# A gated mix of linear attention and a SwiGLU block: the first half of a weight load changes its DMA queue, and one dummy product is dropped

## The chip, the core and the metric

The kernel runs on one core of a Trainium2 chip. The metric is the device time of one execution in microseconds (us). A profile is one further execution of the same program, with a record for each instruction and each DMA.

## The reference

Two branches read the same x and are mixed by a gate for each token. Cut to what matters (S = 2048 tokens, D = 512, F = 1376, 32 heads of 16; all inputs bf16):

```python
g = sigmoid((x * gate_w).sum(-1, keepdims=True))
# A: linear attention, phi(t) = where(t > 0, t + 1, exp(t)) + 1e-6
q, k, v = split(x @ wqkv)                     # each S x 512
kv  = einsum("bhsd,bhse->bhde", phi(k), v);  z = phi(k).sum(over tokens)
a   = (phi(q) @ kv / (phi(q) . z + 1e-6)) @ wo
# B: SwiGLU
b   = (silu(x @ w1) * (x @ w3)) @ w2
out = g * a + (1 - g) * b
```

## The kernel before, in words

The tokens are cut into 16 tiles of 128 (`t`), four tiles to a block of 512 (`tb`). A product on TensorE needs x transposed, with the feature on the partition; this copy is `xT`. Almost all of `xT` is made by transposing DMAs straight from HBM (lines 89 and 93). Only the first two tiles, the "x pair", come in plainly (line 84, 256 KB into `x_sb`) and are turned on TensorE by `emit_xT` (line 176): eight transposes into PSUM, which VectorE (line 181) and ScalarE (line 183) copy into `xT`.

The start of the kernel goes in this order:

- Dummy products (`emit_warm`, line 163) on constants keep TensorE busy while the first loads travel: six of 512 columns and three of 128.
- The eight transposes of the x pair, line 176.
- The k products of tiles 0 to 3 (`emit_k_mm`, line 186): four for each tile, one for each 128-row chunk `kc` of the weight `wk_sb`. The order of the first eight is written out by hand: chunks 0 and 1 of tile 0, chunks 0 and 1 of tile 1, then chunks 2 and 3 of tile 0 and of tile 1. So the first four need only the first half of `wk_sb` (line 85), the next four the second half (line 86). Tiles 2 and 3 read the `xT` that the transposing DMA of line 89 brings.
- From tile 4 on, TensorE alternates between `emit_xp` of tile u (line 206, which reads `x_sb` of tile u) and the k products of tile t. Tiles 2 to 7 of `x_sb` come in one DMA of 768 KB (line 98), and the first of them is wanted by the third `emit_xp`.

After that come the q products, the gate and remainder columns (line 243), the SwiGLU products (lines 312 and 320) and the output products (lines 348 to 357), block by block.

TensorE's order is the order of the program, since the kernel asks for a manual schedule of that engine. Each DMA is issued by an engine's instruction queue, in the order of that queue. All loads but one are issued from SyncE (SP), the exception being line 85, which ScalarE issues:

```python
dq = nc.sync
dq.dma_start(out=x_sb[:, 0:TF, :], in_=x_first)
nc.scalar.dma_start(out=wk_sb[:, 0:2, :], in_=wqkv_r[:, 0:2, D : 2 * D])
dq.dma_start(out=wk_sb[:, 2:4, :], in_=wqkv_r[:, 2:4, D : 2 * D])
```

The whole function:

Of the kernel before, what the change touches and what calls it, by code (L numbers as in the profile page):

```python
# [17 lines left out]
def kernel(  # L18
# [12 lines left out]
    nc = tc.nc  # L31
    P = nc.NUM_PARTITIONS

    Bb, S, D = A_x.shape
# [5 lines left out]
    TB = 512  # L40
# [25 lines left out]
    wk_sb = consts.tile([P, KC, D], BF16, name="wk_sb")  # L66
# [9 lines left out]
    wqkv_r = A_wqkv.rearrange("(kc d) n -> d kc n", d=P)  # L76
# [3 lines left out]
    dq = nc.sync  # L80
# [1 line left out]
    x_first = x2d[0 : TF * P, :].rearrange("(p j) d -> p j d", j=TF)  # L82
    out_first = out2d[0 : TF * P, :].rearrange("(p j) d -> j p d", j=TF)
    dq.dma_start(out=x_sb[:, 0:TF, :], in_=x_first)
    nc.scalar.dma_start(out=wk_sb[:, 0:2, :], in_=wqkv_r[:, 0:2, D : 2 * D])
    dq.dma_start(out=wk_sb[:, 2:4, :], in_=wqkv_r[:, 2:4, D : 2 * D])
    pre = consts.tile([1, 1], FP32, name="pre")
    nc.scalar.activation(out=pre[:], in_=nc.const_aps.tensor(0.0, [1, 1], FP32), func=ACT.Exp)
# [1 line left out]
        out=xT[:, :, TF * P : TB], in_=x2d[TF * P : TB, :], transpose=True  # L90
    )
    for tb in range(1, NTB):
        dq.dma_start(
            out=xT[:, :, tb * TB : (tb + 1) * TB], in_=x2d[tb * TB : (tb + 1) * TB, :],
# [7 lines left out]
    with nc.allow_non_contiguous_dma(reason="one gate weight per partition and chunk"):  # L102
        dq.dma_start(
            out=wr_sb[:, :, 2 * FR : NR], in_=gate_w.rearrange("(kc d o) -> d kc o", d=P, o=1)
# [7 lines left out]
    for fcs in (slice(0, FC // 2), slice(FC // 2, FC)):  # L112
# [9 lines left out]
        out=bm, in_=bm, pattern=[[-Dh, HPC], [0, Dh]], compare_op=ALU.is_ge, fill=0.0,  # L122
# [3 lines left out]
        out=bm, in_=bm, pattern=[[Dh, HPC], [0, Dh]], compare_op=ALU.is_ge, fill=0.0,  # L126
# [33 lines left out]
    def emit_warm(*widths):  # L160
        warm = psX.tile([P, TB], FP32, tag="XP3", name="warm")
        for n in widths:
            nc.tensor.matmul(  # L163
                warm[:, 0:n], lhsT=warm_l, rhs=warm_r[:, 0:n], start=True, stop=True
            )

    emit_warm(TB, TB, TB, TB, TB, TB, P, P, P)

    st = {}

# [244 lines left out]
    for c in range(KC):  # L415
# [7 lines left out]
        out=kvT_sb[:], in0=kvT_ps[:],  # L423
# [65 lines left out]
```

## Time and profile before

| what | value |
|---|---|
| median of 4 runs | 179.68 us (178.89 to 180.21) |
| the profiled execution's own time | 179.26 us |
| its span, from the first to the last instruction | 177.5 us |
| time of that execution outside the span | 1.76 us |
| TensorE busy | 173.0 us, 97% of the span |
| VectorE, ScalarE, GpSimd busy | 66%, 37%, 36% |
| moved by DMA | 15.14 MB, mean 85 GB/s over the span |
| of it from ScalarE's DMA queue (q10) | 0.26 MB |

The span is counted from zero at the first instruction. PE stands for TensorE's products, PEld for its weight loads, which run beside the products; a weight load that waits is named with what it waited for. SPq and ACTq are the DMA-issuing instructions of SyncE and ScalarE; their duration is the time that the issuing engine spends on the instruction, and the time to landing runs from the start of the issue to the last byte's report.

### The profile page before, as it was taken

How to read it: one execution, taken by the hardware profiler on the slowest of the kernel's cores; microseconds unless marked ns; L12 is line 12 of the kernel's file. 1: busy time of each engine (PE TensorE's matmuls, PEld its weight loads, DVE VectorE, ACT ScalarE, POOL GpSimd, SP SyncE). 2: the span in 40 equal slices, each digit the busy share in tenths (PEclk: the TensorE clock that was granted, in tenths of full speed). 3: DMA queues.
4: the chain of work that ended last, by engine and by line, in shares of the span. 5: the costliest groups of instructions: out<-in, count | busy, mean ns of one | idle time of the engine just before them, and what ended most of it. 6: DMA issues, size and time to landing. Idle time of an engine off the chain costs nothing.

```text
span 177.5 us, 2453 instructions
## 1 busy us (share of the span) xinstructions
PE 173.0 (97%) x868; PEld 83.8 (47%) x884; DVE 117.8 (66%) x203; ACT 65.9 (37%) x124; POOL 63.3 (36%) x71
## 2 busy tenths in 40 slices
PE   8999999999999999999999999999999999999993
PEld 4444444474445454444454544444545444444463
DVE  0596858898998637597776466878754668776000
ACT  3624224466433333333244333243434323341222
POOL 5197655958262323262003232710032328000000
PEclk9999999999999999999999999999999999999999
DMA  5999999921014011124000111230002022200011
GB/s 170 230 305 246 234 344 361 350 77 28 9 30 91 7 41 37 37 59 89 0 4 7 40 33 37 71 78 6 0 7 67 7 70 59 59 0 0 30 36 56
DMA packets 30252, 15.14 MB, mean 85 GB/s; under 512 B 20672, under 2 KB 30112, under 8 KB 30240
## 3 DMA queue, kind: packets, MB, share of 16 engines
q1 hardware_dynamic: 29968, 14.72, 30.5%
q10 hardware_dynamic: 272, 0.26, 0.4%
q8 instruction: 7, 0.11, 0.3%
q14 instruction: 5, 0.04, 0.1%
HBM read 8.42 MB, written 2.10 MB: 59 GB/s over the span
## 4 chain that ended last, share of the span: by engine, by line
PE 97%; issue 1%; DVE 0%; DVEq 0%
PE o_ps L357 19%; PE up_ps L320 19%; PE gate_ps L312 19%; PE o_ps L348 8%; PE XP L206 8%; PE q_ps L219 8%; PE k_ps L186 6%; PE r_ps L243 3%; PE k L186 2%; PE o_ps L352 2%; PE warm L163 2%; PE kvT_ps L418 1%; PE W_ps L440 0%; PE xTp L176 0%; PE z_ps L431 0%
## 5 line engine op out<-in xcount | busy, mean ns | idle before, releaser
L312 PE MATMUL gate_ps<-xT,w_sb 128*128 128x512 bf16 x157 | 40.7, 379 | 0.1
L320 PE MATMUL up_ps<-xT,w_sb 128*128 128x512 bf16 x157 | 40.6, 379 | 0.2
L227 POOL TENSOR_TENSOR qz<-pq,z_sb 128x512 f32<-128x512 bf16 x16 | 18.5, 1164 | 59.6 <-DVE pq L147 58.4
L325 ACT ACTIVATE th<-gate_ps 128x512 bf16<-128x512 f32 x40 | 23.9, 597 | 37.9 <-PE gate_ps L312 36.4
L357 PE MATMUL o_ps<-w_sb,hT 128*128 128x512 bf16 (+3 forms) x177 | 37.3, 355 | 0.2
L327 DVE SCALAR_TENSOR_TENSOR gs<-th,gate_ps 128x512 bf16<-128x512 bf16 x40 | 27.3, 683 | 5.6 <-ACT th L325 5.3
L330 DVE TENSOR_TENSOR hT<-up_ps,gs 128x512 bf16<-128x512 f32 x40 | 27.6, 691 | 3.7
L144 DVE TENSOR_SCALAR phi_m<-phi_e 128x512 bf16<-128x512 bf16 x32 | 14.1, 441 | 21.4 <-ACT phi_e L142 21.3
L357 PEld LDWEIGHTS <-hT 128*128 128x128 bf16 x180 | 16.8, 98 | 17.9
L320 PEld LDWEIGHTS <-w_sb 128*128 128x128 bf16 x160 | 15.7, 98 | 18.9
L312 PEld LDWEIGHTS <-w_sb 128*128 128x128 bf16 x160 | 15.6, 98 | 18.6
L362 ACT ACTIVATE o_out<-o_ps,omg 128x512 bf16<-128x512 f32 (+2 forms) x17 | 11.2, 659 | 30.8 <-PE o_ps L357 30.8
L292 POOL TENSOR_TENSOR pqn<-pq,rden 128x512 bf16<-128x512 bf16 x16 | 16.6, 1057 | 14.0 <-DVE rden L285 11.7
L196 POOL TENSOR_TENSOR pks<-pks,pk_sb 128x512 f32<-128x512 f32 x15 | 17.5, 1165 | 7.3 <-DVE pk_sb L147 6.7
L348 PE MATMUL o_ps<-W_sb,pqT 128*128 128x512 bf16 (+3 forms) x70 | 16.7, 354 | 0.1
L230 DVE TENSOR_REDUCE den<-qz 128x32 f32<-128x512 f32 x16 | 11.0, 685 | 8.6 <-POOL qz L227 8.5
L206 PE MATMUL XP<-pk_sb,x_sb 128*128 128x512 bf16 x62 | 16.2, 379 | 0.1
L219 PE MATMUL q_ps<-wq_sb,xT 128*128 128x512 bf16 x61 | 16.1, 379 | 0.1
L142 ACT ACTIVATE phi_e<-k_ps 128x512 bf16<-128x512 f32 x12 | 7.2, 597 | 14.4 <-PE k_ps L186 14.4
L142 ACT ACTIVATE phi_e<-q_ps 128x512 bf16<-128x512 f32 x16 | 9.6, 597 | 7.8 <-PE q_ps L219 6.7
L186 PE MATMUL k_ps<-wk_sb,xT 128*128 128x512 bf16 x48 | 12.3, 379 | 0.0
L147 DVE SCALAR_TENSOR_TENSOR pq<-q_ps,phi_m 128x512 bf16<-128x512 f32 x16 | 11.1, 691 | 0.5
(59 smaller groups left out, 117.1 us busy)
## 6 DMA issues: line engine op xcount, KB each, us to landing
w_sb<-in_B_w_dram SPq DMA_DIRECT2D x6, 640.0 KB, 8.5
out_dram<-o_out SPq DMA_DIRECT2D x15, 128.0 KB, 1.9
x_sb<-in_A_x_dram SPq DMA_DIRECT2D x2, 512.0 KB, 4.2
x_sb<-in_A_x_dram SPq DMA_DIRECT2D x1, 768.0 KB, 5.0
wq_sb<-in_A_wqkv_dram SPq DMA_DIRECT2D x1, 512.0 KB, 6.1
wv_sb<-in_A_wqkv_dram SPq DMA_DIRECT2D x1, 512.0 KB, 6.7
wo_sb<-in_A_wo_dram SPq DMA_DIRECT2D x1, 512.0 KB, 10.1
wk_sb<-in_A_wqkv_dram ACTq DMA_DIRECT2D x1, 256.0 KB, 3.5
```

The costliest lines, as they stand in the source:

```text
L186: nc.tensor.matmul(k_ps[:], lhsT=xT[:, kc, t * P : (t + 1) * P], rhs=wk_sb[:, kc, :], start=(kc == 0), stop=(kc == KC - 1),)
L196: nc.gpsimd.tensor_add(pks[:], pks[:], pk_sb[:, t, :])
L206: nc.tensor.matmul(XP_ps[dc][:], lhsT=x_sb[:, t, dc * P : (dc + 1) * P], rhs=pk_sb[:, t, :], start=(t == 0), stop=(t == NT - 1),)
L219: nc.tensor.matmul(q_ps[:], lhsT=xT[:, kc, ts_tok], rhs=wq_sb[:, kc, :], start=(kc == 0), stop=(kc == KC - 1),)
L227: nc.gpsimd.tensor_tensor(out=qz[:], in0=st[tb, "pq"][:, tt, :], in1=z_sb[:], op=ALU.mult)
L312: nc.tensor.matmul(gate_ps[:], lhsT=w1_sb[:, kc, fsl], rhs=xT[:, kc, tok_sl], start=(kc == 0), stop=(kc == KC - 1),)
L320: nc.tensor.matmul(up_ps[:], lhsT=w3_sb[:, kc, fsl], rhs=xT[:, kc, tok_sl], start=(kc == 0), stop=(kc == KC - 1),)
L325: nc.scalar.activation(out=th[:], in_=gate_ps[:], func=ACT.Tanh, scale=0.5)
L327: nc.vector.scalar_tensor_tensor(out=gs[:], in0=th[:], scalar=1.0, in1=gate_ps[:], op0=ALU.add, op1=ALU.mult)
L330: nc.vector.tensor_tensor(out=st[tb, "hT"][:, fc, :], in0=up_ps[:], in1=gs[:], op=ALU.mult)
L348: nc.tensor.matmul(o_ps[:], lhsT=st[tb, "pqT"][:, c, tsl], rhs=W_sb[:, c, a:b], start=(c == 0), stop=False,)
L357: nc.tensor.matmul(o_ps[:], lhsT=st[tb, "hT"][:, fc, tsl], rhs=w2_sb[:, fc, a:b], start=False, stop=(fc == FC - 1),)
```

## The change

The DMA that loads the first half of `wk_sb` is issued by SyncE instead of ScalarE. In SyncE's queue it stands second, behind the x pair and ahead of the second half of `wk_sb`; whatever SyncE issues after it comes one instruction later than before. The list of dummy products loses one of its three 128-column members.

```diff
     dq.dma_start(out=x_sb[:, 0:TF, :], in_=x_first)
-    nc.scalar.dma_start(out=wk_sb[:, 0:2, :], in_=wqkv_r[:, 0:2, D : 2 * D])
+    dq.dma_start(out=wk_sb[:, 0:2, :], in_=wqkv_r[:, 0:2, D : 2 * D])
     dq.dma_start(out=wk_sb[:, 2:4, :], in_=wqkv_r[:, 2:4, D : 2 * D])
...
-    emit_warm(TB, TB, TB, TB, TB, TB, P, P, P)
+    emit_warm(TB, TB, TB, TB, TB, TB, P, P)
```

## The prediction

> **What bounds the kernel now.** I read the page's chain first, then the start of the span weight load by weight load, then SyncE's DMA issues, then the landings. All of the change lies in the first microseconds; the chain says whether they count.
>
> ```profile
> PEclk9999999999999999999999999999999999999999
> ...
> PE 97%; issue 1%; DVE 0%; DVEq 0%
> ```
>
> The chain that ended last is TensorE's work, almost without a break. So a microsecond that TensorE loses at the start reaches the end in full, and one that it gains does too, if no later load makes it wait. The clock row is for the section on rules below.
>
> The timeline of the weight loads shows what TensorE waits for at the start (start us, length us, line, count, idle before it and its releaser):
>
> ```profile
> 2.93 0.15 PEld L163 LDWEIGHTS <-const-bfloat16-1.0 128*128 128x128 bf16 x1 [0.28 <-issue]
> 3.36 0.25 PEld L163 LDWEIGHTS <-const-bfloat16-1.0 128*128 128x128 bf16 x2 [0.28 <-issue]
> 3.77 0.65 PEld L176 LDWEIGHTS <-x_sb 128*128 128x128 bf16 x8 [0.15 <-DMA x_sb<-in_A_x_dram]
> 4.55 0.11 PEld L186 LDWEIGHTS <-xT 128*128 128x128 bf16 x2
> 4.86 1.10 PEld L186 LDWEIGHTS <-xT 128*128 128x128 bf16 x6 [0.20 <-DVE xT L181]
> 6.32 1.41 PEld L186 LDWEIGHTS <-xT 128*128 128x128 bf16 x8 [0.36 <-DMA xT<-in_A_x_dram]
> ```
>
> Two loads end waits of TensorE: the x pair at 3.77 and the first transposing DMA at 6.32. The second is the one to keep in mind. Between them lie the eight k products of tiles 0 and 1, from 4.55 on, at 0.216 each (the chain has four products of line 206 at 0.86): 4.55 + 8 x 0.216 = 6.28. TensorE and that DMA arrive together, within 0.04; the 0.36 is the idle time of the weight loader, not of the array.
>
> SyncE's DMA issues, in order of time:
>
> ```profile
> 0.81 0.40 SPq L84 DMA_DIRECT2D x_sb<-in_A_x_dram  x1
> 1.27 0.41 SPq L86 DMA_DIRECT2D wk_sb<-in_A_wqkv_dram  x1
> 1.73 1.32 SPq L89 DMA_TRANSPOSE xT<-in_A_x_dram  x1
> 3.10 2.89 SPq L93 DMA_TRANSPOSE xT<-in_A_x_dram  x1
> 6.03 0.58 SPq L98 DMA_DIRECT2D x_sb<-in_A_x_dram  x1
> 6.66 4.17 SPq L93 DMA_TRANSPOSE xT<-in_A_x_dram  x1
> ```
>
> There is no wait between them: SyncE issues as fast as it can, one after the other, so a DMA put in at 1.27 delays the rest. The landings of the DMAs issued by 8 us (KB, us to landing), and, in the second fence, of line 89 alone:
>
> ```profile
> x_sb<-in_A_x_dram SPq DMA_DIRECT2D x1, 768.0 KB, 5.0
> wk_sb<-in_A_wqkv_dram ACTq DMA_DIRECT2D x1, 256.0 KB, 3.5
> x_sb<-in_A_x_dram SPq DMA_DIRECT2D x1, 256.0 KB, 2.9
> wk_sb<-in_A_wqkv_dram SPq DMA_DIRECT2D x1, 256.0 KB, 4.0
> ```
>
> ```profile
> DMA to landing us min/median/max: 4.5/4.5/4.5
> ```
>
> Added to the issue times: x pair 3.71, first half of wk 0.80 + 3.5 = 4.30, second half 5.27, first transposes 6.23, the 768 KB of x 11.03. The user of the last is the third group of line 206:
>
> ```profile
> 11.30 0.31 PEld L206 LDWEIGHTS <-x_sb 128*128 128x128 bf16 x2
> ```
>
> It has no wait, but only 0.27 to spare. Last, the queues while the x pair travels, from 1.5 to 3.35 us (packets, MB, share of the 16 engines):
>
> ```profile
> q1 hardware_dynamic: 143, 0.26, 56.9%
> q10 hardware_dynamic: 117, 0.12, 18.8%
> ```
>
> ScalarE's queue q10 takes 18.8% of the engines' 1.85 us, 0.35 us of each, before the x pair is through.
>
> **The change, part by part.**
>
> *ScalarE loses an issue of 0.45 us* (line 85, at 0.80). Its table load can start half a microsecond earlier, but ScalarE's first real work waits for the transposes until 4.41. Worth nothing; the cover is over 1.5 us.
>
> *The x pair is alone on the engines.* It can land earlier by 0 (q10's packets only fill holes) to 0.35 (all of its share comes back). I take 0.15[...]. TensorE resumes at about 3.62 instead of 3.77.
>
> *The dummy product.* 512 columns step by 0.427 (2.93 to 3.36), so 128 cost about 0.107, an estimate. The dummies end near 3.56 instead of 3.67, just ahead of the earlier x pair. Without this edit the dummies would eat most of the lead; with it nothing is lost unless x comes no earlier, and then TensorE idles 0.1 longer for the same end.
>
> *The first half of wk* is issued at 1.27 instead of 0.80. Its first user runs at 4.55, or 4.40 with the lead. Bounds: 4.30 as now (it follows x in one ring, and the engines are what is short) to 4.77 (0.47 later). At 4.77 the eight products start 0.22 later than now, and all behind them 0.2. I take 4.35, no cost.
>
> *The second half of wk, and the first transposes,* are issued 0.46 later (0.41 for the issue, 0.05 between). The fifth k product wants the second half at 4.55 + 4 x 0.216 = 5.41; it lands at 5.27. Bounds: no shift, if the engines were the limit, to 0.46, which gives +0.32 there and +0.46 at 6.32 for the transposes; these do not add, since both delay the same chain. I take no shift: the bytes ahead of the transposes are the same as before (x and both halves of wk, 768 KB), and line 89 ends its issue at 3.05, long before the second half of wk has landed at 5.27, so its descriptors stand in a backlog. An issue that ends at 3.51 is still 1.8 ahead. So the lead of 0.15 is spent waiting at 6.32: net 0. At best, should the transposes come early too, -0.15.
>
> *The second block's transposes* land at 3.10 + 4.9 = 8.0 and are wanted at 8.71, by the first k product of tile 4. A shift of 0.46 is covered.
>
> *The 768 KB of x* have 0.27 to spare. Shift 0 to 0.46, cost 0 to 0.2. Line 93 spends 2.89 on twice line 89's work of 1.32, so 0.25 of it looks like waiting for room, which the later start may absorb; a shift of some 0.25 is covered. I take 0.05. Later loads: the list of waits names no other DMA that TensorE waits for in the whole span, so 0.46 is hidden there.
>
> Sum: -0.15 at 3.77, +0.15 at 6.32, +0.05 at 11.3: the span goes from 177.5 to 177.55, the profiled time from 179.26 to about 179.3. That execution lies 0.42 below the median of the four; the difference carried over to the median gives 179.7.
>
> **Two rules of the Trainium skill, weighed.** The rows of SyncE's issues show a price of 0.46 for one more issue. "DMA: Bandwidth & Descriptors", section "Issuing engines are not separate DMA queues", says that transfers from all issuing engines share the same 16 DMA engines and that spreading them over engines saves only the issuing time. That speaks against this change: it gives up exactly that saving. If the issue time bound the transposes, they would come 0.46 later and the time be 180.1. The rows speak for a backlog instead, and I keep 179.7.
>
> The clock row prints 9 in all slices, the first too, yet a dummy of 512 columns takes 0.427 and a k product of the same size 0.216: the array ran at half pace at first. Eight transposes take 0.71 in the chain; five at 0.107 and three at 0.054 (quarters of 0.427 and 0.216) make that, so the pace doubled near 4.25, some 3.4 after the first dummy at 0.84. "TensorE: Matmul & The Clock Gate", section on the HAM clock gate, says that full clock comes after a busy window of about 3.4 us, which runs freely and is not started by the kernel. By the row, a hole of about 0.1 (there is one now, from 3.67 to 3.77) did no harm. By the rule a window that is judged not busy costs up to another 3.4 at half pace. The sum by the row is 179.7, by the rule's worst 181.4.
>
> **The rivals.** *Slower: the clock comes late.* Place: from 4.25 on. With one dummy less and x not earlier, TensorE idles 0.2 instead of 0.1 ahead of 3.77; if the window fails for that, TensorE does half its work until about 7.65 and loses up to 1.7. Over 0.9 is lost when the doubling slips by more than 1.8. For it: the runs before spread over 1.3 us, which a floating window could make. Against: the hole now is as large as I expect it after. 180.6 to 181.4.
>
> *The sync queue is the bound.* The 0.46 reaches the transposes, and the 768 KB have more lag than slack: 179.9 to 180.6. For: no waits between SyncE's issues. Against: the backlog.
>
> *Faster:* the transposes follow x and keep the lead, up to 0.35, and the second queue's disuse shortens what lies outside the span, 1.76 us, of which no row shows the parts. To pass 0.9 it would need 0.55 from there: 178.6.
>
> *No effect as told:* x lands at 3.71 as before, q10 having only filled holes. The time is the same 179.7.
>
> **How the numbers follow.** About 0.5%, 0.9 us, is what a measurement of this kernel can tell from no change. Hidden or cancelled, with or without an earlier x: 0.58, at 179.7, of which 0.02 on either side falls past 0.9 by the runs' scatter. Clock late: 0.18. Sync queue the bound: 0.10, of which 0.04 past 0.9. Faster: 0.14. So faster 0.16, same 0.60, slower 0.24. The range takes in the faster case's centre and the lower half of the clock's: 178.6 to 181.0. The likeliest case alone spans 179.2 to 180.2.
>
> **What would show it.** Right: q10 gone; x pair landing near 3.55 and line 176 starting there; the wait for xT in front of tile 2 still ending near 6.3, longer than 0.36; line 206 at 11.3 with a wait of at most 0.1 on the 768 KB. Wrong: tile 2 starting at 6.7 or later (issue-bound), k products stepping by 0.427 past 4.6 (clock), or tile 2 well before 6.2 (the lead kept).

## The result, and the profile after

The changed kernel takes 180.30 us (median of 41 runs, 179.6 to 181.11) against 179.58 us for the kernel before (60 runs, 178.87 to 180.34). The ratio is 1.0036, with a 95% interval of 1.0028 to 1.0045: slower by 0.7 us, a small loss, but clear of zero. It lies in the stated range and within the 0.5% that was given as "same".

The distribution of the runs changed as well. The middle half of the runs before lies between 179.26 and 180.02; that of the changed kernel between 180.18 and 180.39. The change took away the better executions: 43 of the 60 runs before are under 180.0 us, but only 3 of the 41 after it. Its median lies where the slowest runs before lie (180.34), and 13 of its runs lie above them. Any explanation has to cover both, the higher median and the lost better executions.

The profiled execution of the changed kernel took 180.33 us, with a span of 178.5, 1.0 more than before. Its chain, by engine, has gained entries of DMA and SPq:

```profile
PE 90%; DMA 3%; SPq 3%; DVE 1%; issue 1%; ACT 0%; DVEq 0%
```

The chain no longer begins with TensorE: its first 12.5 us are SyncE's issues and one DMA. The timeline of the weight loads shows the places (start us, length us, line, count, idle before and releaser):

```profile
3.50 0.86 PEld L176 LDWEIGHTS <-x_sb 128*128 128x128 bf16 x8
4.38 0.20 PEld L186 LDWEIGHTS <-xT 128*128 128x128 bf16 x2
4.85 0.53 PEld L186 LDWEIGHTS <-xT 128*128 128x128 bf16 x3 [0.27 <-DVE xT L181]
5.70 0.53 PEld L186 LDWEIGHTS <-xT 128*128 128x128 bf16 x3 [0.32 <-issue]
6.81 1.41 PEld L186 LDWEIGHTS <-xT 128*128 128x128 bf16 x8 [0.59 <-DMA xT<-in_A_x_dram]
...
12.58 0.55 PEld L206 LDWEIGHTS <-x_sb 128*128 128x128 bf16 x4 [0.90 <-DMA x_sb<-in_A_x_dram]
```

The x pair is there earlier: line 176 starts at 3.50 without a wait, where it stood at 3.77 with one. Everything after that is later. At 5.70 the fifth k product has waited for the second half of wk, which landed at 5.65 (5.27 before). Tile 2 starts at 6.81 instead of 6.32, after a wait for the first transposes. At 12.58 the third group of line 206, which had no wait before, has waited for the 768 KB of x.

SyncE's issues, and the landings of what was issued by 8 us; the last fence is the landing of line 89 alone:

```profile
1.27 0.41 SPq L85 DMA_DIRECT2D wk_sb<-in_A_wqkv_dram  x1
1.73 0.46 SPq L86 DMA_DIRECT2D wk_sb<-in_A_wqkv_dram  x1
2.23 1.44 SPq L89 DMA_TRANSPOSE xT<-in_A_x_dram  x1
3.72 2.73 SPq L93 DMA_TRANSPOSE xT<-in_A_x_dram  x1
6.49 0.58 SPq L98 DMA_DIRECT2D x_sb<-in_A_x_dram  x1
```

```profile
x_sb<-in_A_x_dram SPq DMA_DIRECT2D x1, 768.0 KB, 6.0
wk_sb<-in_A_wqkv_dram SPq DMA_DIRECT2D x2, 256.0 KB, 3.4
x_sb<-in_A_x_dram SPq DMA_DIRECT2D x1, 256.0 KB, 2.7
```

```profile
DMA to landing us min/median/max: 4.5/4.5/4.5
```

The x pair lands at 0.81 + 2.7 = 3.5. The first transposes need 4.5 us from their issue, as before, but are issued at 2.23, so they land near 6.8; nothing of the 0.5 was made up. Their issue has also grown, from 1.32 to 1.44. The 768 KB need 6.0 us instead of 5.0, on top of an issue 0.46 later: 12.5 instead of 11.0.

### The profile page after: what moved, and what is told of

It reads as the page before. It is cut to its first block, busy times and chain, and to the rows that moved or that the text cites. A ratio compares the mean times of both kernels' runs of the same rounds, so it can differ in the third digit from the quotient of the medians.

```text
span 178.5 us, 2451 instructions
## 1 busy us (share of the span) xinstructions
PE 173.5 (97%) x867; PEld 83.9 (47%) x883; DVE 118.7 (66%) x203; ACT 66.0 (37%) x124; POOL 63.1 (35%) x71
## 4 chain that ended last, share of the span: by engine, by line
PE 90%; DMA 3%; SPq 3%; DVE 1%; issue 1%; ACT 0%; DVEq 0%
PE o_ps L357 19%; PE up_ps L320 19%; PE gate_ps L312 19%; PE o_ps L348 8%; PE q_ps L219 8%; PE XP L206 6%; PE k_ps L186 4%; DMA x_sb<-in_A_x_dram 3%; PE r_ps L243 3%; PE o_ps L352 2%; SPq L93 2%; SPq L89 1%; DVE phi_m L144 1%; PE kvT_ps L418 1%; PE W_ps L440 0%
## 5 line engine op out<-in xcount | busy, mean ns | idle before, releaser
L144 DVE TENSOR_SCALAR phi_m<-phi_e 128x512 bf16<-128x512 bf16 x32 | 15.1, 473 | 21.6 <-ACT phi_e L142 21.5
```

## The experiments

The theories are called A and B in the first two sets and R, I and P in the last. Theory A put the loss on the 768 KB of x, Theory B on the first microseconds. All ratios are against the kernel before.

**The two parts alone.** The move with all nine dummies:

```diff
-    emit_warm(TB, TB, TB, TB, TB, TB, P, P)
+    emit_warm(TB, TB, TB, TB, TB, TB, P, P, P)
```

> The move of the wk load alone, with all nine dummy products as before. Theory A (the 768 KB of x is the late one: it is issued about 0.46 us later and lands near 12.5 us, and TensorE waits for it in front of the third group of line 206): the dropped dummy is worth nothing, so the time is that of the changed kernel, ratio to before about 1.004, with that block landing past 12 us. Theory B (what is lost is lost at the very start: dummies, clock and the first products): the longer dummy stretch changes the start by about 0.1 us and may bring the full clock earlier, ratio 1.000 to 1.002.

Measured 1.0049 (1.0033 to 1.0064). The move alone carries the loss, but, in its one profile, not by Theory A's way: the first transposes land at 6.9 and tile 2 starts at 6.94, and the 768 KB cost nothing (a wait of 0.16 of the weight loader, none of the products). That execution took 179.87, among the quickest of this kernel. Five of its 22 runs lie at 181.0 to 181.4, in no profile; they lift the ratio (the median, 180.21, is no higher than the changed kernel's), and what they wait for is not shown.

The kernel before with the dummy dropped, the same edit of that line in the other direction:

> One short dummy product fewer alone; the first half of wk stays on the ScalarE queue. Theory A: no difference, ratio 1.000 (0.999 to 1.001), the 768 KB of x landing near 11.0 us as before. Theory B (the shorter dummy stretch lets the full clock come late): slower, ratio 1.002 to 1.004, with k products stepping by 0.427 us past 4.6 us in more executions than before.

Measured 0.9987 (0.9973 to 1.0001). The dummy is worth nothing that can be told from zero, and it is not what slows the kernel.

**One more SyncE issue, without moving wk.** Added to the kernel before:

```diff
     nc.scalar.dma_start(out=wk_sb[:, 0:2, :], ...)
+    spare = consts.tile([P, 64], BF16, name="spare")
+    dq.dma_start(out=spare[:], in_=x2d[0:P, 0:64])
     dq.dma_start(out=wk_sb[:, 2:4, :], ...)
```

> The kernel before, with one more DMA on the SyncE queue at the place in question: 16 KB into a tile that nothing reads, added work. The first half of wk stays on the ScalarE queue, so that only SyncE's later issues move by some 0.45 us, and no load-bearing bytes change queue. Theory A in the form that the issue time does it: the first transposes land about 0.45 us later, the 768 KB of x at 11.5 to 12.5 us, ratio 1.002 to 1.004. Rival (the bytes of wk in SyncE's rings do it, the issue being covered by the backlog): the landings stay at 6.3 and 11.0 us, ratio 1.000.

Measured 1.0028 (1.0016 to 1.0040): most of the loss comes with 16 KB that nobody reads. In this one profile, though, the transposes were on time (issue 2.19, landing 6.20) and only the 768 KB came late, 6.1 us after their issue. That execution, at 179.71, was one of the quickest of this kernel (179.65 to 180.72).

**The 768 KB from ScalarE.**

```diff
-        dq.dma_start(out=x_sb[:, x_ts, :], in_=x_r[:, x_ts, :])
+        if tb > 1:
+            dq.dma_start(out=x_sb[:, x_ts, :], in_=x_r[:, x_ts, :])
...
     emit_xT(1)
+    nc.scalar.dma_start(out=x_sb[:, TF : 2 * TPB, :], in_=x_r[:, TF : 2 * TPB, :])
```

> The changed kernel, with the 768 KB of x (tiles 2 to 7) issued by ScalarE after the copies of the x pair, near 5.1 us, instead of by SyncE at 6.5 us. Theory A: the block lands before 11.3 us, the wait in front of the third group of line 206 goes, what is left is the wait for the first transposes (about 0.5 us later than before), and the ratio falls from 1.004 to about 1.000 to 1.002. Theory B (the start is what is lost, about 1 us by 9 us): ratio stays at 1.004. A third outcome: the block shares the engines with the second block's transposes and delays those past 8.7 us, ratio above 1.004.

Measured 1.0221 (1.0190 to 1.0252): above 1.004 as in the third outcome, but not in the way told there. The timeline of ScalarE, and of the weight loads, says why (line 187 there is line 186 of the kernel before):

```profile
0.86 0.44 ACTq L380 DMA_DIRECT2D x_sb<-in_A_x_dram  x1
```

```profile
7.18 0.10 PEld L187 LDWEIGHTS <-xT 128*128 128x128 bf16 x1 [2.65 <-issue]
7.46 0.15 PEld L187 LDWEIGHTS <-xT 128*128 128x128 bf16 x1 [0.19 <-issue]
7.89 0.15 PEld L187 LDWEIGHTS <-xT 128*128 128x128 bf16 x1 [0.28 <-issue]
```

The load waits for nothing, so it was put at the head of ScalarE's queue, at 0.86 instead of the 5.1 that was meant. Its 768 KB went ahead of wk, whose first half needed 5.9 us to land; the weight loader stood for 2.65, and TensorE then ran k products at 0.43 a step instead of 0.216. As a test of Theory A it failed; it shows what this early large load on the second queue cost.

**The third group of line 206 one tile later,** in both kernels:

```diff
-        for u in range(n_xp, n_xp + (2 if t == NT - 4 else 1)):
+        for u in range(n_xp, n_xp + {TPB: 0, NT - 5: 2, NT - 4: 2}.get(t, 1)):
```

> The changed kernel with TensorE's order shifted: the first group of line 206 comes one tile later (none ahead of the k products of tile 4, and two groups ahead of those of tiles 11 and 12 each), so the 768 KB of x are wanted 0.86 us later; the same work in all. Theory A (the wait for the 768 KB, 0.57 us in the changed kernel's profile, is the last one and carries the loss): the wait in front of the third group is under 0.1 us and the ratio falls from 1.004 to about 1.001 to 1.003, what is left being the wait for the first transposes. Theory B (the loss is made by the second half of wk and the first transposes, by 6.8 us): ratio stays at 1.003 to 1.005.

> The same shift of line 206 in the kernel before. Its runs lie in two heaps, near 179.25 and near 180.05 us. If the upper heap is executions in which the 768 KB of x come late (Theory A), it goes: median about 179.2 us, ratio 0.997 to 0.999. If the heaps come from the start (clock, transposes), both stay and the ratio is 0.999 to 1.001.

Measured 1.0028 (1.0015 to 1.0040) for the changed kernel and 1.0002 (0.9985 to 1.0019) for the one before. With the 768 KB wanted 0.86 later, most of the loss stays and the scatter of the runs before stays. Theory A falls as the main cause: the late 768 KB of the first profile were that execution's last wait, not the rule.

**Both kernels once more,** for a second profile of each:

> The changed kernel once more, for a second profile of it. Theory A: again the second half of wk past 5.4 us, the first transposes near 6.8 us and the 768 KB of x at 12 us or later. If these landings vary from one execution to the next, another of the three will be the last wait.

> The kernel before once more, for a second profile of it. Both theories expect the second half of wk near 5.3 us and the first transposes near 6.3 us again; if the execution falls in the upper heap (near 180.05 us), Theory A expects the 768 KB of x past 11.6 us in it.

They took 180.35 and 180.12. The second profile of the changed kernel has the 768 KB in time for its group and the start still later: second half of wk at 6.26, first transposes at 7.36, tile 2 at 7.39. The second profile of the kernel before is the other surprise. All its loads landed as in the first (second half of wk 5.25, transposes 6.26, 768 KB 11.08), and it is 0.86 us slower all the same. Its weight loads:

```profile
5.00 0.15 PEld L186 LDWEIGHTS <-xT 128*128 128x128 bf16 x1 [0.28 <-DVE xT L181]
5.43 0.15 PEld L186 LDWEIGHTS <-xT 128*128 128x128 bf16 x1 [0.28 <-issue]
5.86 0.15 PEld L186 LDWEIGHTS <-xT 128*128 128x128 bf16 x1 [0.28 <-issue]
6.28 0.15 PEld L186 LDWEIGHTS <-xT 128*128 128x128 bf16 x1 [0.28 <-issue]
6.62 2.04 PEld L186 LDWEIGHTS <-xT 128*128 128x128 bf16 x10 [0.19 <-issue]
```

The k products step by 0.43 until about 6.5: in this execution the array got its full pace 2.3 us later than in the first, whose doubling was near 4.25. Tile 2 starts at 7.26.

**What makes the transposes late.** By now five profiles had SyncE issue the transposes as its fourth DMA; in four of them these landed at 6.77 to 7.36. (The kernel with the 768 KB on ScalarE is left out of this count, since those bytes went ahead.) Theory R: with both halves of wk in SyncE's queue, some DMA engines finish the second half late, and the transposes behind it. Theory I: one more issue ahead of the transposes does it. Four kernels, the last the most telling: the second half of wk from ScalarE instead of the first (the transposes are SyncE's third DMA again); the 16 KB kernel with line 206 one tile later; both halves from ScalarE; and both halves in one SyncE load, which leaves all 768 KB ahead of the transposes on SyncE but makes the transposes its third DMA.

```diff
 # swap: the changed kernel with
-    dq.dma_start(out=wk_sb[:, 2:4, :], ...)
+    nc.scalar.dma_start(out=wk_sb[:, 2:4, :], ...)
 # both: the kernel before with the same line on nc.scalar
 # merged: the changed kernel with
-    dq.dma_start(out=wk_sb[:, 0:2, :], ...)
-    dq.dma_start(out=wk_sb[:, 2:4, :], ...)
+    dq.dma_start(out=wk_sb[:], in_=wqkv_r[:, :, D : 2 * D])
```

> The changed kernel, but the second half of wk is issued by ScalarE; the first half stays on SyncE. SyncE issues as many loads as in the kernel before. Theory R (with both halves of wk in SyncE's queue a few engines finish the second half late, and the first transposes behind it): second half landed by 5.3 us, first transposes by 6.35, ratio 0.999 to 1.001. Rival theory P (the order of the first half decides, since it starts only when the x pair is through): the transposes stay at 6.8 us or later, ratio 1.002 to 1.005.

> The 16 KB load on SyncE ahead of the second half of wk (later issues only, wk's first half on ScalarE) together with the later order of line 206. Theory R: the issue time moves neither the second half of wk (5.1 to 5.3 us) nor the first transposes (6.2 to 6.3), and with the 768 KB wanted 0.86 us later their lateness is hidden too: ratio 0.999 to 1.001, against 1.0028 without the later order. Theory I (0.45 us of issue time by itself makes the transposes late, the one profile of that kernel having been a lucky one): transposes at 6.7 or later, ratio 1.002 to 1.004.

> Both halves of wk issued by ScalarE, SyncE issuing only the x pair ahead of the transposes; nine dummies. Theory R: the transposes are issued near 1.27 us and land at 6.3 us or before, ratio 0.998 to 1.001; it cannot gain much, since TensorE was level with the transposes in the kernel before. Rival (the two halves of wk share the engines with the transposes now and land later, past 5.5 us): ratio 1.002 to 1.005.

> The changed kernel with both halves of wk in one load of 512 KB on SyncE, so that the first transposes are issued near 1.73 us, as in the kernel before, with the same bytes ahead of them in SyncE's queue as in the changed kernel. The first k product now waits for all of wk. Theory R: wk ends late (past 5.4 us) and the transposes land at 6.7 us or later, though they are issued on time. Theory I: the transposes land at 6.2 to 6.35 us. The time tells less: with wk whole near 5.3 us the eight products end near 7.1 us, ratio 1.002 to 1.004; with wk later, up to 1.006.

Merged: issued at 1.73, landed at 6.21, all of wk at 5.21. So both halves of wk in one queue are not the cause that Theory R took them for: the same bytes through one queue are on time. Swap: transposes at 6.20. Both: at 6.28. The 16 KB kernel: at 7.03, with the second half of wk at 6.02, though half of wk is on ScalarE's queue. This is what Theory I expected of the merged and the 16 KB kernel, and the 16 KB kernel's first profile was not its rule. The issue of the transposes in the 16 KB kernel, in the profile that was on time and in the one that was late (line 91 there is line 89 of the kernel before):

```profile
2.19 1.32 SPq L91 DMA_TRANSPOSE xT<-in_A_x_dram  x1
```

```profile
2.20 1.66 SPq L91 DMA_TRANSPOSE xT<-in_A_x_dram  x1
```

The times: swap 1.0060 (1.0028 to 1.0092), 16 KB with the later order 1.0031 (1.0017 to 1.0046), both 1.0020 (1.0007 to 1.0033), merged 1.0048 (1.0028 to 1.0068). Swap and merged are slow for another reason, which their profiles show: the first k product starts at 5.3 instead of 4.5, since in the swap ScalarE's second half lands ahead of the first (which lands at 5.29), and in the merged kernel all of wk must be there. Four of the 12 runs of the swap, at 181.6 to 182.3, and one of the merged kernel, at 181.8, are in no profile, and their cause is not shown.

What the DMA engines did meanwhile shows in the stretches 5.0 to 5.5 and 5.5 to 6.0. First the second profile of the changed kernel, then the merged one (us, PE, PEld, DVE, ACT and POOL busy, clock, DMA share, GB/s):

```profile
5.00:5.50 0.50, 0.50 (x3) 0.15 (x1) 0.00 (x0) 0.05 (x1) 0.00 (x0) 1.00 1.49 52
5.50:6.00 0.50, 0.46 (x2) 0.10 (x1) 0.00 (x0) 0.00 (x0) 0.00 (x0) 1.00 0.07 23
```

```profile
5.00:5.50 0.50, 0.24 (x1) 0.10 (x1) 0.00 (x0) 0.15 (x1) 0.00 (x0) 1.00 1.27 283
5.50:6.00 0.50, 0.50 (x2) 0.15 (x1) 0.00 (x0) 0.00 (x0) 0.00 (x0) 1.00 1.30 256
```

In the changed kernel the packets begun in the second stretch carry 23 GB/s, with the transposes issued since 2.23 and part of wk still to come. The kernel before has 268 and 272 there. The engines are not idle, though. A packet's time is counted where it begins, and the 1.49 of the first stretch belongs to packets that run on through the second. These are packets of the transposes: in the trace, 19 packets of 256 bytes begin between 4.59 and 5.40, take 0.70 to 1.50 us each (0.018 is usual), and all end between 6.08 and 6.12. What the engines begin in the meantime is this (GB/s in 40 slices from 5.5 to 6.0, and the packets by size):

```profile
GB/s 82 0 0 0 82 0 0 82 0 0 0 82 0 0 82 0 0 82 0 0 0 82 0 0 82 0 0 0 82 0 0 21 0 20 20 20 20 20 20 20
DMA packets 18, 0.01 MB, mean 23 GB/s; under 512 B 9, under 2 KB 18, under 8 KB 18
```

An 82 is one packet of 1 KB in its slice (1024 bytes in 0.0125 us), and at this time only wk has packets of that size: nine of them, one at a time. So the transposes, whose first packet began at 4.12, wait while the last packets of wk go through; the last one ends at 5.90, and the 19 packets 0.2 later. That one DMA engine works off its share of wk while the others wait for it would fit this spacing, but the trace does not name the engines. In twelve of the thirteen profiles of the table below, late or not, the transposes land 1.44 to 1.49 us after the end of wk's last packet (1.62 in the other). What comes late is the end of wk, and the transposes follow it. In that much Theory R was right.

**All profiles in one table.** Times in us, read from the trace; "tile 2" is the start of its first k product.

| kernel | last packet of wk ends | transposes issued, landed | full pace from about | tile 2 | execution | execution less tile 2 |
|---|---|---|---|---|---|---|
| before | 4.83 | 1.73, 6.28 | 4.2 | 6.32 | 179.26 | 172.94 |
| before, second profile | 4.81 | 1.73, 6.26 | 6.5 | 7.26 | 180.12 | 172.86 |
| dummy only | 4.86 | 1.73, 6.31 | 4.4 | 6.35 | 179.31 | 172.96 |
| later order, before | 4.80 | 1.72, 6.25 | 5.3 | 6.63 | 179.49 | 172.86 |
| both from ScalarE | 4.79 | 1.26, 6.28 | 6.5 | 7.30 | 180.34 | 173.04 |
| swap | 4.75 | 1.72, 6.20 | 3.9 or before | 7.05 | 179.91 | 172.86 |
| merged | 4.73 | 1.73, 6.21 | 6.3 | 7.48 | 180.48 | 173.00 |
| changed | 5.30 | 2.23, 6.77 | 4.8 | 6.81 | 180.33 | 173.52 |
| changed, second profile | 5.90 | 2.23, 7.36 | 5.4 | 7.39 | 180.35 | 172.96 |
| move only | 5.45 | 2.23, 6.90 | 4.4 | 6.94 | 179.87 | 172.93 |
| later order, changed | 5.73 | 2.23, 7.18 | 4.0 | 7.21 | 180.35 | 173.14 |
| 16 KB | 4.58 | 2.19, 6.20 | 4.1 | 6.24 | 179.71 | 173.47 |
| 16 KB, later order | 5.59 | 2.20, 7.03 | 6.0 | 7.06 | 180.08 | 173.02 |

The last column is one number, 172.86 to 173.14, in all but two; in those two the 768 KB of x came 6.0 us or more after their issue, and TensorE lost another half microsecond to them. So the execution's time is the start of tile 2 plus a constant, and tile 2 starts at the latest of three things: the k products of tiles 0 and 1 (which depend on when the array gets its full pace), the first k products' own loads, and the first transposes. In the kernel before, the transposes at 6.3 decide when the pace comes early, and the pace when it comes late: tile 2 starts anywhere from 6.3 to 7.3. In the changed kernel, the move alone and the later order, the transposes at 6.8 to 7.4 decide in all four profiles, and a late pace is hidden in the wait for them. That gives both facts of the result: the higher median, and the lost better executions. The runs above 180.9 us of the move alone, the swap and the merged kernel are not covered by it.

No kernel here beat the one before by more than its interval.

## Why the prediction was right or wrong

- *The verdict* (same, by the bound of 0.5%) and the range held; the central 179.7 was 0.6 short. That was luck in good part. The margin to the bound was small, 0.36% of 0.5%, and the case that came is not the likeliest one but, in place and size, the rival *the sync queue is the bound*, with its 179.9 to 180.6 and its chance of 0.10. Its sign, tile 2 at 6.7 or later, is in both profiles of the changed kernel (6.81 and 7.39). The way there was another, as the fifth point says.
- *The x pair* was to gain 0.15. It landed at 3.46 instead of 3.72, its first weight load came 0.27 earlier (3.50 against 3.77) and its first product 0.20 (3.57), inside the bounds of 0 and 0.35. That q10's packets held it up is likely but not clean: it landed at 3.43 to 3.65 in the five profiles without them, at 3.53 to 3.85 in the eight with them, the kernel with the 768 KB on ScalarE left out. As foreseen, the lead was spent waiting in front of tile 2.
- *ScalarE's freed issue* and *the first half of wk* cost nothing: that half landed at 4.1 to 4.4 in the two profiles of the changed kernel, the move alone and the later order, and the first k product ran at 4.4 to 4.5.
- *The dummy* at nothing: right, 0.9987 (0.9973 to 1.0001) alone.
- *The second half of wk and the first transposes:* this is the step that failed. It took no shift because the bytes ahead were the same and the descriptors stood in a backlog, with an upper bound of 0.46. The bytes alone are indeed no cause (the merged kernel), but in these four profiles the transposes landed 0.5 to 1.1 later and the second half of wk 0.4 to 1.0 later (5.65 to 6.26 against 5.27). The bound itself was too low: it let a later issue shift the landing by no more than the issue. The backlog itself was there: the issue ended at 3.7 to 3.8, and the transposes' first packets began at 4.1 to 4.4, against 4.2 to 4.3 in the kernel before. What the sum left out is that the backlog stands behind the end of wk, and that this end can move: 5.30 to 5.90 instead of 4.83.
- *The 768 KB* at 0.05, bounds 0 to 0.2: on average small (1.0036 against 1.0028 with the later order, whose intervals overlap), but 0.57 of TensorE in one profile, because the landing took 6.0 instead of 5.0. The longer time to landing had no place in the sum.
- *The rule against the change,* from the Trainium skill, "DMA: Bandwidth & Descriptors", section "Issuing engines are not separate DMA queues": a second issuing engine saves only issue time. I weighed it and set it aside; the 180.1 that it gave was nearer than my 179.7. Even it was short: the landings moved by up to 1.1, more than twice the issue time of 0.46, so in these runs the choice of the engine was worth more than its issue time.
- *The clock rival* had the mechanism but the wrong kernel. The pace doubles anywhere from 3.9 or before to 6.5 in these profiles. The Trainium skill, "TensorE: Matmul & The Clock Gate", Part 1 on the HAM clock gate, has a freely running window that makes this point vary by 0.5 us to either side. The traces agree that the point varies, but by 2.6 us in all, and their measure decides; the window itself no trace here shows. In the kernel before and its two variants that are as quick, the time follows it (pace from 4.2, 4.4, 5.3 and 6.5; 179.26, 179.31, 179.49 and 180.12 us), which makes it the cause of most of the scatter before. The second profile before has the same dummies and the same gap as the first, so no larger gap is needed for a late pace. In the changed kernel it is hidden: the rival's sign, k products stepping by 0.427 past 4.6, is in the second profiles of both kernels and does not tell them apart.
- *Carrying over the 0.42* between the profiled execution and the median took a difference between two kinds of execution for a constant: the profile before was one of the early-pace executions, and in those the transposes weigh more than in the others. From this profile alone the loss would be 0.5 to 1.1; over the runs it is 0.7, since late-pace executions lose little.

What stays open: what draws out the end of wk, and whether it is the number of SyncE's issues ahead of the transposes or their instant. In the second profile of the changed kernel one packet of wk, begun at 3.93, takes 1.34 us (0.046 is usual), but in the move alone none takes over 0.3 us, and wk ends late all the same. The runs show that the lateness goes with the transposes' own issue (1.31 to 1.33 long where they land on time, 1.44 to 1.66 where late), and that it happened in five of the six profiles (again without the 768 KB on ScalarE) in which they were the fourth DMA of SyncE and in none of the seven where they were the second or third. Open too is why the 768 KB took 6 us in two profiles. There again it is the end: in the first profile of the changed kernel 740 of their 768 packets were through by 11.04, the last 28 only by 12.14. The kernel with both halves from ScalarE is 0.2% slower than before with its transposes on time; its x pair landed 0.1 later (3.82), which accounts for a part at most.

## What to carry to other kernels

Where TensorE and a load arrive within 0.04 us of each other, ask how much later the load can come, and do not take "the bytes ahead are the same" for an answer: here the order and number of issues on the queue counted beside the bytes. Look at the end of the load that goes ahead, packet by packet, and not only at when the waiting load was issued. Take a second profile before you build a sum on the first, when the runs scatter by more than the effect: here the same kernel was bound by the array's pace in one execution and level with a DMA in the other. And subtract a landmark (here the start of tile 2) from each execution's time; if the rest is constant, the difference lies ahead of it.

## What the runs showed of the hardware

- The clock row on the pages of the kernel before and of the changed one printed 9 from the first slice on, while dummies and k products stepped by 0.427 until as late as 6.5 us. The pace had to be read from the steps.
- 16 KB more on one issuing queue delayed a transposing DMA that came after it by 0.75 us (7.03 against 6.28) in one execution and by nothing in another.
- Of two 256 KB loads on different queues, the one on ScalarE's went first (landed 4.52, against 5.29 for SyncE's, in the swap), though SyncE's was issued only 0.46 later; SyncE's stood behind the x pair, which landed at 3.85.
- Packets of a transposing DMA were held at the engines, up to 1.50 us instead of 0.018, until the last packets of the plain load ahead of it were through; the DMA landed 1.44 to 1.49 us after the last of these in twelve of thirteen profiles.
